# Four edits in the opening steps of a fused attention, FFN and routed-expert kernel, and one rule on when the routing search may advance

## The chip, the cores and the metric

The kernel runs on one core of one Trainium2 chip. The metric is the device time of one execution in microseconds, as the median of several runs; below 0.2% (about 1.6 us here) two kernels can hardly be told apart. A core has TensorE (PE; its weight loads are shown as PEld), VectorE (DVE), ScalarE (ACT), GpSimd (POOL) and SyncE (SP), each with its own instruction stream in program order. They wait for one another by semaphores. Matmul results land in PSUM banks; everything else lies in SBUF.

## The reference, cut to what matters

```python
# 1. retention attention: q, k, v are (4, 8, 576, 64)
ret = (scale * q @ k.T) * Dmat            # Dmat: decay gamma**(i-j) below the diagonal
x = (ret @ v)                             # -> x: 2304 tokens x 512
# 2. a dense FFN over all tokens
h = x @ w_in                              # 512 -> 2048
g = h * np.tanh(np.log1p(np.exp(h)))
x = g @ w_out                             # 2048 -> 512
# 3. routing: 8 experts with room for 288 tokens each
logits = x @ w_gate
order = np.argsort(-logits.flatten())     # greedy: the best (token, expert) pair first,
                                          # skipping taken tokens and full experts
# 4. each expert's FFN on its own 288 rows
out[mask] = np.maximum(x[mask] @ w1[e], 0.0) @ w2[e]    # 512 -> 1024 -> 512
```

## The kernel before, in words

**First part.** `first_part` runs attention and the dense FFN together. The tokens are cut into 9 blocks of 256 and the 2048 features into 16 tiles; a step is one pair (block, tile). Every product is made from a high and a low half of each operand: `ff_h` does 12 products into `ph` (4 contraction tiles, each xh·winh, xh·winl, xl·winh, L323). Then a step walks through short passes: `ff_a1` (three ACT passes on `d`, L332 to L334, and a DVE product `rs`, L340), `ff_a2` (DVE reciprocal, L345), `ff_b1` (DVE product `u`, L350), `ff_b2` (DVE, L358) and `ff_b3` (high half `gh` on ACT, L364; low half `gl` on DVE in these steps, L365). Three steps later `ff_y` multiplies by w_out.

**Weights.** They arrive as raw words and are converted, one 128x512 part per step over the first 32 parts, by the methods of `convert`: `x1` (L163) and `c` (L160) on ACT at the end of a step, `x` (L167) and `a` (L172) on DVE at the start of the next, `h` on ACT (L178, the high half `winh`/`woh`), and one step later `l` (L181, the low half `winl`/`wol`) on POOL. `c` writes a tile `y` in SBUF, and `a` combines `y` with the raw words, which also lie in SBUF.

**Attention pieces.** `slots` hangs the attention of the next tokens into the steps. `a_scores(c)` makes the scores of chunk c in two PSUM banks and their decayed copies `pm` (DVE, L228), and scales Q and K in place on POOL (L232, L237). `a_out(c)` multiplies: four products with the state `sd` (L247), eight with `pm` (L252); then the block's input is written as `xh` (ACT, L258) and `xl` (DVE, L259). `a_state(c)` updates the state bank F (L277). PSUM banks A to E are handed out in turn by `bank()`. Step 4 is block 1 with tile 0, the first step that needs block 1's xh and xl, which `a_out(3)` in step 3 completes. Within step 3 the source has, in this order: `x` and `a` of the part in work, `u` of step 2, `ff_a1` of step 3, `gh`/`gl` of step 1, then the slots, then `ff_h` of step 4.

**Second part.** The experts run one after the other, `ph` 0 to 7: 96 products into `hp` (L1336), then 96 into `op` (L1350), all with 288 columns. A planner in the program text keeps an estimated clock of each engine (`clk`) and decides between products which side piece is put in next: `step()`, a piece of the routing search (`cnt` L1045, `full` L1049, `dg` L1055, `tau` L1060, `ind` L728 on DVE; at the end of an expert's search `de` L1064 on PE and a DVE chain from `dm` L1066 to `m0n` L1075), `fill()` (building the row lists), the gather of the next expert's rows, and `transposes(ph + 1, kt)`, four of them (`tps` counts them): three transposes `tp` on PE (L1297, two buffers), then `xth` on ACT (L1310) and `xtl` on DVE (L1314). A `step()` moves the planner's clocks, so where it is taken decides what the planner does later too.

Of the kernel before, what the change touches and what calls it, by code (L numbers as in the profile page):

```python
# [7 lines left out]
F32 = mybir.dt.float32  # L8
# [4 lines left out]
U32 = mybir.dt.uint32  # L13
U16 = mybir.dt.uint16
I64 = mybir.dt.int64
AF = mybir.ActivationFunctionType
ALU = mybir.AluOpType

P = 128
B, H, S, D = 4, 8, 576, 64  # L20
N, DM, FF, E, F = 2304, 512, 2048, 8, 1024
# [9 lines left out]
MID = (2, 3, 5, 8, 8, 9, 11, 14)  # L31
JOIN = (9, 14)
YL = 3
NF = FF // P


# [45 lines left out]
def first_part(ctx, tc, att, att_ht, att_hn, dtab, qtab, ktab, stab, wi, wo, wgb, ydram, L, constants, cst, begin, grid):  # L82
    nc = tc.nc
# [9 lines left out]
    D_ = big.tile([P, 2, 4, P], F32, name="dt")  # L93
# [49 lines left out]
    class convert:  # L143
# [8 lines left out]
            self.i = done[0]  # L152
            done[0] += 1

        def c(self):
            if self.i in (2, 3):
                self.t = spare[:, self.i % 2 * 512:][:, :512]
            else:
                self.t = cvs[self.i % 2]
            nc.scalar.activation(self.t, self.w1.bitcast(F32), AF.Copy, scale=2.0 ** -112)  # L160

        def x1(self):
            nc.scalar.activation(self.w0, self.top, AF.Copy, scale=2.0 ** -13, bias=-0.4999)  # L163
# [1 line left out]
        def x(self):  # L165
            w0 = self.w0
            nc.vector.scalar_tensor_tensor(w0, self.w1, 0x80000000, w0, op0=ALU.bitwise_and,  # L167
                                           op1=ALU.bitwise_or)

        def a(self):  # L170
            t = self.t.bitcast(U32)
            nc.vector.scalar_tensor_tensor(t, t, 3, self.w0, op0=ALU.logical_shift_left,  # L172
                                           op1=ALU.bitwise_or)
            if self.i not in (6, 7):
                fetch()
# [18 lines left out]

    att_tags = ["A", "B", "C", "D", "E"]
    turn = [0]

    def bank(tag=None):  # L200
# [93 lines left out]
    def micro(n):  # L294

        out = []
        for ci in chunks_of(n):
            if n == 3:
                out.append([lambda ci=ci: a_scores(ci, (0,))])
                out.append([lambda ci=ci: a_scores(ci, (1,))])  # L300
            else:
                out.append([lambda ci=ci: a_scores(ci)])
            out.append([lambda ci=ci: a_out(ci)])
            out.append([lambda ci=ci: a_state(ci),
                        lambda ci=ci: load_chunk(ci + 2) if ci + 2 < len(CHUNKS) else None])
        return out
# [8 lines left out]
    def ff_h(n, f, i):  # L315
        xh, xl = x_block(n)
        if i % 2 == 0:
            hbank[0] = psum.tile([P, 2, TB], F32, tag=("ph0", "ph1")[i // 2 % 2], name="ph")
        ph = hbank[0][:, i % 2, :]
        k = 0  # L320
        for kt in range(KT):
            for w, x in ((winh, xh), (winl, xh), (winh, xl)):
                nc.tensor.matmul(ph, w[f][:, kt, :], x[:, kt, :], start=(k == 0), stop=(k == 11))  # L323
                k += 1
        q2[n, f] = ph
# [160 lines left out]
    slots = {}  # L486
# [14 lines left out]
        nc.tensor.matmul(state[0][:, hp % 4, :], SD[:, 0, :], SD[:, 0, :], start=True, stop=True)  # L501
    unread = psum.tile([P, 2, TB], F32, tag="ph1", name="unread")

    def fill(n):
        for k in range(n):
            nc.tensor.matmul(unread[:, 0, :P], D_[:, 0, 0, :], D_[:, 0, 1, :], start=True, stop=True)

    a_scores(0)
    fill(2)
# [50 lines left out]
    for i in range(len(steps) + YL):  # L560
        new = i < len(steps)
        if not i or new and not_yet(i):
            ff_h(*steps[i], i)
        if i == 20:
            constants()
        if i == 62:
            stage.__exit__(None, None, None)
            late = tc.tile_pool(name="late", bufs=1)
            WG = late.__enter__().tile([P, E, DM], F32, name="WG")
            nc.sync.dma_start(WG, wgb)  # L570
        if now:
            now.x()
            now.a()
        if old:
            old.l()
        if new:
            n, f = steps[i]
            alone = bool(now or old)
            eng = nc.vector if alone else nc.gpsimd
            if not alone:  # L580
                for x in slots.get(i, []):
                    x()
            if i and steps[i - 1] in inv:
                ff_b1(*steps[i - 1], nc.vector)
            ff_a1(n, f, i, alone)
            if i > 1:
                ff_b3(*steps[i - 2], eng)
            if alone:
                for x in slots.get(i, []):
                    x()  # L590
            if now:
                now.h()
            if alone or i == len(steps) - 2:
                ff_h(*steps[i + 1], i + 1)
            while behind:
                behind.pop()()
            ff_a2(n, f)
            if i:
                ff_b2(*steps[i - 1])
            if eng is not nc.vector:  # L600
                ff_b1(n, f, nc.vector if i == len(steps) - 1 else eng)
        if i == len(steps) - 1:
            ff_b2(n, f)
            ff_b3(*steps[i - 1], nc.gpsimd)
            ff_b3(n, f, nc.vector)
        old, now = now, None
        if nxt and i in CONV:
            now, nxt = nxt, convert() if done[0] < len(parts) else None
            now.x1()
            now.c()  # L610
        for k in range(2 if i % 4 == 0 or TAIL <= i < POP2 else 1):
            if idle:
                idle.pop(0)()
        if late and i > TAIL + BEGIN and not idle:
            late = late.__exit__(None, None, None)
            soon.extend(begin())
        if i >= YL:
            ff_y(*steps[i - YL], i)
# [18 lines left out]
RM = (0, 0.1)  # L637
# [165 lines left out]
def second_part(ctx, tc, L, ydram, wx, cst, out, st, fast, L0=None):  # L803
# [5 lines left out]
    nc = tc.nc  # L809
# [642 lines left out]
    for ph in range(E):  # L1452
# [12 lines left out]
        for i, _ in enumerate(ffn(ph)):  # L1465
            clk["pe"] += MM
            rush()
            hurry = fills and ph + 1 not in IDX
            if hurry:
                if fills[0][0] or clk["dve"] <= clk["pe"] + HB:  # L1470
                    fill()
            elif len(COMP) < ph + 3 and clk["route"] + RM[ph > 0] <= clk["pe"]:
                step()
            elif fills and clk["dve"] <= clk["pe"] + 0.7:
                fill()
            if gat and ph + 1 in IDX:
                gather(ph + 1)
                clk["pool"] = max(clk["pool"], clk["pe"], clk["dve"] + 0.9) + 3.5
                there = clk["pool"] + 2.3
                gat = False  # L1480
            fetch()
            if fetched and fetched[0][0] <= ph + 1 and fetched[0][3] + DD <= clk["pe"] \
                    and clk["pool"] <= clk["pe"] + 1.0 \
                    and (not hurry or max(clk["pool"], clk["pe"] + 1.0) + 2.35 <= clk["gather"] + DG):
                split()
            if i in DUE:
                pieces(ph, DUE[i])
            if i in todo:
                todo[i]()
            if nxt and not gat and i >= due and tps < KT and clk["pe"] >= there:  # L1490
                transposes(ph + 1, tps)
                tps += 1
                due = i + min(20, max(6, (188 - i) // max(KT - tps, 1)))
# [145 lines left out]
```

## Time and profile before

| what | value |
|---|---|
| median of 3 runs | 793.83 us (793.38 to 793.94) |
| the profiled execution, whole | 800.43 us |
| its span (first to last instruction) | 798.6 us |
| PE busy | 756.1 us, 95% |
| DVE busy | 541.0 us, 68% |
| ACT busy | 435.2 us, 54% |
| POOL busy | 483.3 us, 61% |
| mean granted clock of TensorE | 0.977 |

The profiled execution is 6.60 us longer than the median; 1.83 us of it lies outside the span. A share of 95% is an average over stages. So the profile is read by stretches: in a stretch where PE isn't full, another engine sets the pace, and in the others PE does. A row of the timeline gives the start in us, the duration, the engine, the line, the operation, out<-in with the shapes, the count, and in brackets the idle time of that engine before the row with what ended it. Instructions on one engine overlap a little, so the distance of two starts is the cost of the first one.

### The profile page before, as it was taken

How to read it: one execution, taken by the hardware profiler on the slowest of the kernel's cores; microseconds unless marked ns; L12 is line 12 of the kernel's file. 1: busy time of each engine (PE TensorE's matmuls, PEld its weight loads, DVE VectorE, ACT ScalarE, POOL GpSimd, SP SyncE). 2: the span in 40 equal slices, each digit the busy share in tenths (PEclk: the TensorE clock that was granted, in tenths of full speed). 3: DMA queues.
4: the chain of work that ended last, by engine and by line, in shares of the span. 5: the costliest groups of instructions: out<-in, count | busy, mean ns of one | idle time of the engine just before them, and what ended most of it. 6: DMA issues, size and time to landing. Idle time of an engine off the chain costs nothing.

```text
span 798.6 us, 16299 instructions
## 1 busy us (share of the span) xinstructions
PE 756.1 (95%) x6163; PEld 698.4 (87%) x6163; DVE 541.0 (68%) x1260; ACT 435.2 (54%) x944; POOL 483.3 (61%) x546
## 2 busy tenths in 40 slices
PE   7799899999999999999999999949999999999995
PEld 6687777898989998989889999839899989999995
DVE  5999998555646897997988976666566754542220
ACT  4789997545445545555555564414444644644631
POOL 2643333555546676676675665327688988978921
PEclk9999999999999999999999999958999999999998
DMA  9556442010333200212010000045466567556411
GB/s 344 201 180 217 158 146 75 28 31 24 106 99 114 80 27 27 81 54 80 16 38 27 2 27 2 1 160 189 145 190 189 172 200 221 164 165 218 136 31 32
DMA packets 27380, 87.79 MB, mean 110 GB/s; under 512 B 4464, under 2 KB 5616, under 8 KB 27168
## 3 DMA queue, kind: packets, MB, share of 16 engines
q1 hardware_dynamic: 24160, 77.06, 29.7%
q0 software_dynamic: 3136, 9.64, 3.7%
q8 instruction: 49, 0.80, 0.4%
q14 instruction: 35, 0.29, 0.1%
HBM read 77.25 MB, written 9.44 MB: 109 GB/s over the span
## 4 chain that ended last, share of the span: by engine, by line
PE 72%; DVE 13%; issue 7%; POOL 2%; ACT 2%; DMA 2%; another core or an unknown queue 0%; POOLq 0%; SPq 0%; DVEq 0%; ACTq 0%
PE ph L323 20%; PE hp L1336 10%; PE op L1350 10%; PE b_E L417 8%; PE b_F L417 8%; DVE rs L345 3%; DVE y L172 2%; DVE raw L167 2%; PE cnt L1045 1%; PE b_A L223 1%; DVE u L350 1%; POOL wxl L876 1%; PE b_D L252 1%; PE b_E L453 1%; PE b_F L453 1%
## 5 line engine op out<-in xcount | busy, mean ns | idle before, releaser
L323 PE MATMUL ph<-xh,winh 128*128 128x256 f32 x576 | 164.9, 286 | 8.4 <-ACT d L332 5.4
L323 PE MATMUL ph<-xl,winh 128*128 128x256 f32 x576 | 160.7, 279 | 0.8 <-DVE xl L259 0.8
L323 PE MATMUL ph<-xh,winl 128*128 128x256 f32 x576 | 160.8, 279 | 0.0
L876 POOL TENSOR_TENSOR wxl<-wraw,wxh 128x1024 fp32r<-128x1024 f32 x63 | 149.3, 2394 | 9.0 <-ACT wxh L874 7.5
L323 PEld LDWEIGHTS ph<-xh,winh 128*128 128x128 f32 x576 | 108.5, 188 | 23.8 <-ACT d L332 9.9
L365 POOL TENSOR_TENSOR gl<-u,gh 128x256 fp32r<-128x256 f32 x114 | 88.9, 780 | 62.9 <-ACT gh L364 62.2
L332 ACT ACTIVATE d<-ph 128x256 f32<-128x256 f32 x144 | 54.9, 381 | 128.8 <-PE ph L323 114.5
L323 PEld LDWEIGHTS ph<-xh,winl 128*128 128x128 f32 x576 | 108.6, 189 | 4.0
L345 DVE RECIPROCAL u<-u 128x128 f32<-128x128 f32 x113 | 107.7, 953 | 3.9
L323 PEld LDWEIGHTS ph<-xl,winh 128*128 128x128 f32 x576 | 108.6, 189 | 1.3 <-DVE xl L259 1.3
L340 DVE TENSOR_TENSOR u<-d 128x128 f32<-128x128 f32 x113 | 53.4, 473 | 60.6 <-ACT d L334 60.0
L352 POOL TENSOR_TENSOR u<-d,u 128x128 f32<-128x128 f32 x112 | 51.7, 461 | 58.8 <-DVE u L345 58.8
L333 ACT ACTIVATE d<-d,half_b 128x256 f32<-128x256 f32 x144 | 73.5, 511 | 4.7
L874 ACT ACTIVATE wxh<-wraw 128x1024 fp32r<-128x1024 f32 x64 | 67.3, 1053 | 13.6 <-DMA wraw<-in_wx_dram 13.6
L353 POOL TENSOR_TENSOR u<-d,u 128x128 f32<-128x128 f32 x112 | 68.8, 614 | 8.8
L334 ACT ACTIVATE d<-d 128x256 f32<-128x256 f32 x144 | 60.2, 418 | 4.5
L364 ACT ACTIVATE gh<-u 128x256 fp32r<-128x256 f32 x144 | 58.1, 403 | 5.4 <-DVE u L358 4.4
L374 DVE SCALAR_TENSOR_TENSOR scr<-y,WG 128x512 bf16<-128x512 f32 x64 | 56.4, 881 | 0.4
L1327 DVE SCALAR_TENSOR_TENSOR htl<-hp,hth 128x288 fp32r<-128x288 f32 x64 | 29.1, 455 | 35.1 <-ACT hth L1339 34.2
L358 DVE SCALAR_TENSOR_TENSOR u<-u,ph 128x256 f32<-128x256 f32 x144 | 52.0, 361 | 0.0
L1339 ACT ACTIVATE hth<-hp 128x288 fp32r<-128x288 f32 x64 | 26.1, 409 | 43.4 <-PE hp L1336 34.5
L1336 PE MATMUL hp<-xth,wxh 128*128 128x288 f32 x256 | 49.4, 307 | 0.0
(299 smaller groups left out, 1874.6 us busy)
## 6 DMA issues: line engine op xcount, KB each, us to landing
wraw<-in_wx_dram SPq DMA_DIRECT2D x64, 512.0 KB, 4.4
att<-in_att_dram SPq DMA_DIRECT2D x32, 512.0 KB, 5.8
raw<-in_wi_dram SPq DMA_DIRECT2D x16, 512.0 KB
raw<-in_wo_dram SPq DMA_DIRECT2D x16, 512.0 KB, 3.2
ydram<-y SPq DMA_DIRECT2D x9, 512.0 KB, 2.8
WG<-in_wgb_dram SPq DMA_DIRECT2D x1, 2048.0 KB
att<-in_att_ht_dram SPq DMA_DIRECT2D x4, 256.0 KB
att<-in_att_hn_dram SPq DMA_DIRECT2D x4, 256.0 KB
```

Source lines behind the costliest of these rows:

```text
L323: nc.tensor.matmul(ph, w[f][:, kt, :], x[:, kt, :], start=(k == 0), stop=(k == 11))
L333: nc.scalar.activation(df, df, AF.Square, bias=half_b, scale=-0.5)
L334: nc.scalar.activation(df, df, AF.Copy, bias=0.5, scale=0.5)
L345: nc.vector.reciprocal(r, r)
L353: eng.tensor_mul(u[:, 0, :], d[:, 1, :], r)
L364: nc.scalar.activation(gh, g, AF.Copy)
L365: eng.tensor_sub(gl, g, gh.bitcast(F32))
L417: nc.tensor.matmul(py[n][t], g[:, t * P:(t + 1) * P], w[f], start=(f == 0 and w is woh and g is gh), stop=(f == NF - 1 and g is gl))
L874: nc.scalar.activation(hi, raw, AF.Copy)
L876: rest = lambda eng: eng.tensor_sub(lo, raw, hi.bitcast(F32))
L1336: nc.tensor.matmul(hp, W[ft // 2][w][:, s], x[:, kt, :], start=(k == 0), stop=(k == 11))
L1350: nc.tensor.matmul(op, W[4 + dt][w][:, s], h[:, ft, :], start=(k == 0), stop=(k == 23))
```

## The change

Five edits, four in the first part:

1. A constant `SOON = 3` names the step. The PSUM bank E is kept out of the rotation of the attention pieces until step 4, so that the early pieces take A to D.
2. `c(aside)`: at the end of steps 0 and 1 ACT writes the converted part to PSUM bank E instead of `y`. In steps 1 and 2 DVE's `a` then reads one input from PSUM and one from SBUF, and writes `y`.
3. The K scaling of chunk 3 goes from POOL to DVE.
4. In step 3, `ff_a1` and the slots (`a_out(3)`, `a_state(3)`, a load) stand ahead of `u` and `gh`/`gl`; six products that nobody reads, into bank E, stand between the slots and `ff_h` of step 4.
5. In the second part `step()` is not taken while `ph == 0` and at least one of the second expert's four transposes has been put in.

```diff
@@ -31,6 +31,7 @@
 YL = 3
+SOON = 3
@@ -152,12 +153,13 @@
-        def c(self):
+        def c(self, aside=False):
             if self.i in (2, 3):
                 self.t = spare[:, self.i % 2 * 512:][:, :512]
             else:
                 self.t = cvs[self.i % 2]
-            nc.scalar.activation(self.t, self.w1.bitcast(F32), AF.Copy, scale=2.0 ** -112)
+            self.s = bank("E").rearrange("p a b -> p (a b)") if aside else self.t
+            nc.scalar.activation(self.s, self.w1.bitcast(F32), AF.Copy, scale=2.0 ** -112)
@@ -168,8 +170,7 @@
         def a(self):
-            t = self.t.bitcast(U32)
-            nc.vector.scalar_tensor_tensor(t, t, 3, self.w0, op0=ALU.logical_shift_left,
+            nc.vector.scalar_tensor_tensor(self.t.bitcast(U32), self.s.bitcast(U32), 3, self.w0, op0=ALU.logical_shift_left,
                                            op1=ALU.bitwise_or)
@@ -194,7 +195,7 @@
-    att_tags = ["A", "B", "C", "D", "E"]
+    att_tags = ["A", "B", "C", "D"]
@@ -299,7 +300,7 @@
-                out.append([lambda ci=ci: a_scores(ci)])
+                out.append([lambda ci=ci: a_scores(ci, eng=nc.vector if ci == 3 else nc.gpsimd)])
@@ -501,9 +502,9 @@
-    def fill(n):
+    def fill(n, to=unread[:, 0, :P]):
         for k in range(n):
-            nc.tensor.matmul(unread[:, 0, :P], D_[:, 0, 0, :], D_[:, 0, 1, :], start=True, stop=True)
+            nc.tensor.matmul(to, D_[:, 0, 0, :], D_[:, 0, 1, :], start=True, stop=True)
@@ -561,6 +562,8 @@
+        if i == SOON + 1:
+            att_tags.append("E")
@@ -577,17 +580,22 @@
-            if not alone:
-                for x in slots.get(i, []):
-                    x()
+            todo = list(slots.get(i, []))
+            if i == SOON:
+                ff_a1(n, f, i, alone)
+            if not alone or i == SOON:
+                while todo:
+                    todo.pop(0)()
             if i and steps[i - 1] in inv:
                 ff_b1(*steps[i - 1], nc.vector)
-            ff_a1(n, f, i, alone)
+            if i != SOON:
+                ff_a1(n, f, i, alone)
             if i > 1:
                 ff_b3(*steps[i - 2], eng)
-            if alone:
-                for x in slots.get(i, []):
-                    x()
+            while todo:
+                todo.pop(0)()
+            if i == SOON:
+                fill(6, bank("E")[:, 0, :])
@@ -607,7 +615,7 @@
-            now.c()
+            now.c(i < 2)
@@ -1469,7 +1477,7 @@
-            elif len(COMP) < ph + 3 and clk["route"] + RM[ph > 0] <= clk["pe"]:
+            elif len(COMP) < ph + 3 and clk["route"] + RM[ph > 0] <= clk["pe"] and (ph or not tps):
                 step()
```

Lines of the changed kernel stand 1 or 2 higher in the first part and 8 higher in the second. Three places show the moved instructions.

On DVE, steps 2 and 3 of the first part, before (`raw` and `y` are the converted part, `rs` and `u` the gate, `att` chunk 3's K):

```order
L167 SCALAR_TENSOR_TENSOR raw<-raw 128x512
L172 SCALAR_TENSOR_TENSOR y_153<-y_153,raw 128x512
L350 TENSOR_TENSOR u<-d,rs 128x256
L340 TENSOR_TENSOR rs<-d 128x128
L365 TENSOR_TENSOR gl<-u,gh 128x256
L228 TENSOR_TENSOR pm<-b_E,dt 128x512
L228 TENSOR_TENSOR pm<-b_A,dt 128x512
L345 RECIPROCAL rs<-rs 128x128
L358 SCALAR_TENSOR_TENSOR u<-u,ph 128x256
L167 SCALAR_TENSOR_TENSOR raw<-raw 128x512
L172 SCALAR_TENSOR_TENSOR y_153<-y_153,raw 128x512
L350 TENSOR_TENSOR u<-d,rs 128x256
L340 TENSOR_TENSOR rs<-d 128x128
L365 TENSOR_TENSOR gl<-u,gh 128x256
L259 TENSOR_TENSOR xl<-b_B,xh 128x4x128
```

The same stretch of DVE after:

```order
L169 SCALAR_TENSOR_TENSOR raw<-raw 128x512
L173 SCALAR_TENSOR_TENSOR y_153<-b_E,raw 128x512
L351 TENSOR_TENSOR u<-d,rs 128x256
L341 TENSOR_TENSOR rs<-d 128x128
L366 TENSOR_TENSOR gl<-u,gh 128x256
L229 TENSOR_TENSOR pm<-b_B,dt 128x512
L229 TENSOR_TENSOR pm<-b_C,dt 128x512
L238 TENSOR_TENSOR att<-att,kt 128x512
L346 RECIPROCAL rs<-rs 128x128
L359 SCALAR_TENSOR_TENSOR u<-u,ph 128x256
L169 SCALAR_TENSOR_TENSOR raw<-raw 128x512
L173 SCALAR_TENSOR_TENSOR y_153<-y_153,raw 128x512
L341 TENSOR_TENSOR rs<-d 128x128
L260 TENSOR_TENSOR xl<-b_D,xh 128x4x128
L351 TENSOR_TENSOR u<-d,rs 128x256
```

The first `y` pass reads the bank E, the K scaling stands behind the two `pm`, and `xl` stands ahead of `u` and `gl` where it stood behind both.

On PE, the end of the first expert (its last `op` products, then the second expert's first `hp`; `tp` are the second expert's transposes), before:

```order
L1297 MATMUL tp<-c_ident,xg 128x96 x3
L1350 MATMUL op<-hth,wxl_6887 128x288
L1055 LDWEIGHTS c_ones
L1055 MATMUL dg<-cl,c_ones 128x1
L1350 MATMUL op<-hth,wxl_6887 128x288 x3
L1350 MATMUL op<-htl,wxh_6886 128x288 x2
L1297 MATMUL tp<-c_ident,xg 128x96 x3
L1350 MATMUL op<-htl,wxh_6886 128x288 x6
L1297 MATMUL tp<-c_ident,xg 128x96 x6
L1336 MATMUL hp<-xth,wxh_7029 128x288
L1045 LDWEIGHTS ind
L1045 MATMUL cnt<-oh,ind 66x8
```

The same place on PE after:

```order
L1305 MATMUL tp<-c_ident,xg 128x96 x3
L1358 MATMUL op<-hth,wxl_6896 128x288 x4
L1358 MATMUL op<-htl,wxh_6895 128x288 x2
L1305 MATMUL tp<-c_ident,xg 128x96 x3
L1358 MATMUL op<-htl,wxh_6895 128x288 x6
L1305 MATMUL tp<-c_ident,xg 128x96 x6
L1344 MATMUL hp<-xth,wxh_7038 128x288
L1063 LDWEIGHTS c_ones
L1063 MATMUL dg<-cl,c_ones 128x1
L1344 MATMUL hp<-xth,wxh_7038 128x288 x3
```

The `dg` of the search moves from before the turns' end to behind the first `hp` product, and with it `tau`, `ind` (DVE) and the next 18 `cnt` products.

On PE, the end of the second expert (`tp` are now the third expert's transposes, `de` the end of the third expert's search), before, where the four turns stand at distances of some 13 products:

```order
L1297 MATMUL tp<-c_ident,xg 128x96 x3
L1350 MATMUL op<-hth,wxh_7327 128x288
L1064 LDWEIGHTS c_ones
L1064 MATMUL de<-full,c_ones 128x8
L1350 MATMUL op<-hth,wxh_7327 128x288 x3
L1350 MATMUL op<-hth,wxl_7328 128x288 x8
L1350 MATMUL op<-htl,wxh_7327 128x288
L1297 MATMUL tp<-c_ident,xg 128x96 x3
```

The same place on PE after:

```order
L1305 MATMUL tp<-c_ident,xg 128x96 x3
L1358 MATMUL op<-htl,wxh_7352 128x288
L1072 LDWEIGHTS c_ones
L1072 MATMUL de<-full,c_ones 128x8
L1358 MATMUL op<-htl,wxh_7352 128x288 x4
L1305 MATMUL tp<-c_ident,xg 128x96 x9
L1344 MATMUL hp<-xth,wxh_7401 128x288 x4
```

The first turn stands some 40 products later than before, and the other three behind one another right ahead of the third expert's first product. On DVE the four `xtl` (L1322) stand together behind `dm` to `m0n`; before, one stood ahead, and the others apart. From the fifth expert on, the order of the second part is the one before. The POOL stream has one instruction less (K), SP's is the same.

## Rows read from the trace of the kernel before

**Rows 1.** Windows: stretch, length, busy PE, PEld, DVE, ACT, POOL; PEclk, DMA, GB/s.

```profile
60.00:80.00 20.00, 18.54 (x138) 15.70 (x137) 19.47 (x41) 18.81 (x43) 7.01 (x7) 1.00 0.60 215
140.00:160.00 20.00, 20.00 (x130) 17.88 (x130) 11.97 (x23) 11.21 (x28) 11.62 (x20) 1.00 0.08 28
```

**Rows 2.** Timeline of DVE, steps 1 to 3.

```profile
14.01 0.70 DVE L237 TENSOR_TENSOR att<-att,kt 128x512 f32<-128x512 f32 x1
...
22.18 0.68 DVE L228 TENSOR_TENSOR pm<-b_B,dt 128x512 f32<-128x512 f32 x1
...
25.05 1.58 DVE L172 SCALAR_TENSOR_TENSOR y<-y,raw 128x512 uint32<-128x512 uint32 x1
...
28.93 0.69 DVE L167 SCALAR_TENSOR_TENSOR raw<-raw 128x512 uint32<-128x512 uint32 x1
29.73 1.61 DVE L172 SCALAR_TENSOR_TENSOR y<-y,raw 128x512 uint32<-128x512 uint32 x1
31.27 1.26 DVE L350 TENSOR_TENSOR u<-d,rs 128x256 f32<-128x256 f32 x1
32.45 1.35 DVE L340 TENSOR_TENSOR rs<-d 128x128 f32<-128x128 f32 x1
...
35.26 0.94 DVE L345 RECIPROCAL rs<-rs 128x128 f32<-128x128 f32 x1
...
37.79 0.42 DVE L350 TENSOR_TENSOR u<-d,rs 128x256 f32<-128x256 f32 x1
38.12 0.29 DVE L340 TENSOR_TENSOR rs<-d 128x128 f32<-128x128 f32 x1
```

**Rows 3.** Timeline of POOL, the same steps.

```profile
22.08 1.32 POOL L232 TENSOR_TENSOR att<-att,qt 128x512 f32<-128x512 f32 x1
...
24.36 1.73 POOL L181 TENSOR_TENSOR winl<-spare,winh 128x512 fp32r<-128x512 f32 x1
...
28.94 1.85 POOL L232 TENSOR_TENSOR att<-att,qt 128x512 f32<-128x512 f32 x1 [0.28 <-POOL wol L181]
30.74 1.51 POOL L237 TENSOR_TENSOR att<-att,kt 128x512 f32<-128x512 f32 x1
32.21 1.45 POOL L181 TENSOR_TENSOR wol<-y,woh 128x512 fp32r<-128x512 f32 x1
```

**Rows 4.** Timeline of PE: products that waited, in steps 1 and 3.

```profile
23.45 1.16 PE L247 MATMUL b_D<-att,sd 128*128 128x128 f32 x8 [1.19 <-POOL att L232]
...
34.80 0.43 PE L252 MATMUL b_B<-pm,att 128*64 128x128 f32 x2 [2.46 <-DVE pm L228]
...
39.40 0.39 PE L323 MATMUL ph<-xl,winh 128*128 128x256 f32 x1 [0.46 <-DVE xl L259]
```

**Rows 5.** Windows behind PE's waits of 1.19 and 2.46 us; columns as above.

```profile
23.40:26.00 2.60, 2.55 (x40) 2.39 (x40) 2.50 (x4) 1.32 (x4) 2.60 (x2) 1.00 0.90 359
...
36.00:37.50 1.50, 1.50 (x23) 1.50 (x21) 1.40 (x4) 0.52 (x2) 0.00 (x0) 0.50 0.00 0
```

**Rows 6.** Timelines of PE, then DVE, at the first expert's end.

```profile
573.54 0.47 PE L1297 MATMUL tp<-c_ident,xg 96*128 96x96 f32 x3 [0.64 <-DVE xtl L1314]
```

```profile
572.24 0.77 DVE L728 TENSOR_TENSOR ind<-dv,tau 128x594 bf16<-128x594 f32 x1
```

**Rows 7.** Timelines of PE, then DVE, at the second expert's end.

```profile
599.88 0.18 PE L1064 MATMUL de<-full,c_ones 66*128 66x8 bf16 x1
...
600.40 1.22 PE L1350 MATMUL op<-hth,wxl 128*128 128x288 f32 x8
```

```profile
600.11 0.17 DVE L1066 TENSOR_REDUCE dm<-de 128x1 f32<-128x8 f32 x1 [1.04 <-PE de L1064]
...
601.19 0.45 DVE L1314 TENSOR_TENSOR xtl<-tp,xth 128x288 fp32r<-128x288 f32 x1
```

**Rows 8.** Timeline of PE and a window, early in the fourth expert's phase.

```profile
649.97 0.17 PE L1064 MATMUL de<-full,c_ones 66*128 66x8 bf16 x1 [1.93 <-DVE full L1049]
...
650.00:653.40 3.40, 3.40 (x17) 3.37 (x17) 2.52 (x13) 2.14 (x4) 2.44 (x4) 0.53 0.40 116
```

## The prediction, made before the changed kernel had run

> **What bounds the kernel now.** I read the windows first. Between 60 and 80 us DVE is busy 19.47 of 20 us and ACT 18.81, while PE has gaps, 18.54; between 140 and 160 us PE is busy all 20 and DVE only 11.97 [rows 1]. So the early steps are paced by DVE with ACT close behind, and all later ones by PE. An opening that brings DVE's chain forward by some time therefore passes that time on to the end; one that only fills PE's gaps there does not. Then I read the timelines of DVE and POOL side by side. A pass of DVE with two SBUF inputs of 128x512 takes 0.70 us when POOL is idle (the row at 14.01) [rows 2]. `a` takes 1.58 at 25.05 and 1.61 at 29.73, and ends where a POOL pass ends: `winl` runs 24.36 to 26.09, Q 28.94 to 30.79 [rows 2, 3]. Q, which began while DVE's `x` (28.93 to 29.62) was running, took 1.85 instead of 1.32. So each blocks the other for a whole pass, whichever began first. `u` at 31.27 and `rs` at 32.45 take 1.26 and 1.35 in the same way, and 0.42 and 0.29 later, when POOL has stopped [rows 2]. A pass that reads PSUM and SBUF isn't held: `pm` at 22.18 takes 0.68 while Q runs from 22.08 [rows 2, 3]. PE pays for this with 2.46 us ahead of `a_out(3)` and 0.46 ahead of the first product with xl [rows 4]. Last I read the ends of the first two experts, where edit 5 works [rows 6, 7].
>
> **Edits 2 and 1: `a` reads PSUM.** The nearest row for the new form is `pm`, unheld at 0.68; the farthest is today's 1.61. I take 0.69, since `pm` is the same mix of sources beside the same kind of POOL pass. The Trainium skill, "VectorE: DVE Perf Modes", section "The TRN2 errata", lists a PSUM source at 120 fixed cycles against 58 at 0.96 GHz; as an estimate that makes two passes 0.13 us longer and the time 0.13 us worse. The trace shows no such difference: `pm` takes 0.68, the SBUF form 0.70 [rows 2], so nothing is added for it.
>
> The replay, step by step:
> - Step 1: `a` would end 0.9 earlier, but `u` behind it, which began when `a` had ended (26.6), has two SBUF inputs and is held until `winl` ends at 26.09. What is left is 0.5, and `x` of step 2 starts at 28.43 instead of 28.93.
> - Step 2: POOL's Q can begin when `x` lets go, near 29.1, and ends 1.3 later, at 30.4 (1.32 when unheld) [rows 3]. `a` runs 29.2 to 29.9, not held. `u` is held by Q until 30.4 and ends some 0.25 behind it, near 30.6 (before: 32.53, where POOL's K ended at 32.25). `rs` takes 0.29 instead of 1.35. Then `gl` (0.4) and the two `pm` (0.6 apart each) as before. The reciprocal that started at 35.26 could start at 32.3: 3.0 us earlier.
> - **Edit 3.** K on DVE adds 0.60 to 0.70 to this chain (the row at 14.01) [rows 2], and POOL's `wol` (1.28 to 1.45) may hold it a little, 0.2. It takes K's 1.51 off POOL [rows 3], which DVE no longer has to wait for. The reciprocal then starts near 33.05: a gain of **2.2**.
>
> **Edit 4.** `a_out(3)` starts when the second `pm` ends, near 32.3 instead of 35.3, so PE's wait of 2.46 goes. `xl` now stands ahead of `u` and `gl`, 0.42 and 0.4 of work that it no longer waits for. DVE is back to back there, so moving passes about doesn't shorten its chain: the gain at the next reciprocal stays 2.2. ACT's `gh` and `xh` follow those DVE and PE rows, and come earlier with them. The six products have 128 columns each, at most 0.14 us a piece by the eight in 1.16 at 23.45 [rows 4], so 0.6 to 0.9 in all. They lie in a gap: with some 1.7 us (an estimate from the same row, for more but smaller products) PE would be done with `a_out(3)` and `a_state(3)` near 34.0. xl comes later: `rs` at 38.12 started 2.86 behind the reciprocal at 35.26 [rows 2]; without `u` (0.33) ahead and with `rs` itself (0.2), xl starts 2.7 behind the new reciprocal, at 35.8, and ends near 36.4. So the six cost nothing while xl is late; if it came by 34.0, they would cost all of their 0.9. What is left of the gap is a pause of about 1.4 us ahead of the third product. PE's granted clock was 1.00 in the stretch of the 1.19 us wait and 0.50 behind the 2.46 us one [rows 4, 5]. The new pause is nearer the first, so I take full clock; at half clock for about 2 us PE loses 1 us, partly hidden since DVE paces. The opening then gives 2.2, with bounds of 0.8 (half clock and `gl` held) and 3.0 (K free).
>
> **Edit 5, end of the first expert.** Before, PE waits 0.64 us ahead of the fourth turn for an `xtl`, which stood behind the `ind` pass of 0.77 at 572.24 [rows 6]. Without search pieces between the turns this `ind` is gone from there and `xtl` follows its `xth` directly. I leave 0.2 for the short chain from `xth`, and let the 18 `cnt` products behind move without loss: **-0.5** (bounds 0 and -0.8). What is not searched here must be searched later; in the later experts PE is the bound and the search passes hide beside its products, so the pieces cost what they cost now.
>
> **Edit 5, end of the second expert.** The planner's clocks have moved: the third expert's four turns stand together, 39 products later. On DVE their `xtl` stand behind `dm` to `m0n`. That chain runs from `de` at 599.88 to the `xtl` at 601.19: 1.31 us [rows 7]. Before, it ran beside a dozen products, eight of which take 1.22 (the row at 600.40) [rows 7], and PE did not wait. After, only four products (0.6) stand between `de` and the nine transposes, and there are two buffers, so the third turn waits for the first `xtl`: 1.31 + 0.45 (a pass) - 0.6 - 0.2 (three transposes) = 1.0 (0.96). The fourth turn waits 0.2 more, the first products of the third expert 0.2. Against it stand some 0.3 for interruptions saved. Net **+1.0** (bounds +0.6 and +1.7). The gather stands as many products ahead of its first turn as before, so I give it nothing.
>
> **Waits behind `full`.** `de` at 649.97 waited 1.93, and the clock after it was 0.53 over 3.4 us [rows 8], a loss of 1.6. Such waits come while POOL issues gathers. Edit 5 reorders the search there. Whether they go, stay, or appear elsewhere can't be read from the order; bounds -3.5 and +3.5, and I take 0, as the nearest row of the same instruction, `de` at 599.88, waited for nothing.
>
> **Sum.** -2.2 - 0.5 + 1.0 = **-1.7**. The profiled execution becomes 800.43 - 1.7 = 798.7. It stood 6.6 above the median, and I keep that distance: 793.83 - 1.7 = **792.1**.
>
> **Rivals.**
> - **The race (792.9 to 793.3).** Where DVE's `gl` or K begins just after POOL's `wol`, it is held for up to 1.2 us: by the replay `gl` starts only some 0.2 us before `wol` does. The Trainium skill, "SBUF — State Buffer", section "Who interferes with whom", says that whoever begins first has the shared ports for the whole instruction, which the rows at 25.05 and 28.94 agree with. The opening then gives 1.0, and with -0.5 and +1.0 the sum is -0.5: 793.3. For it: 0.2 us is less than the replay's error. Against: `gl` goes first as drawn.
> - **The change doesn't do it (793.5).** `a` from PSUM is still held, as its second input lies in SBUF. Then edits 2 and 3 give only what K's move gives, 1.51 of POOL less against 0.6 of DVE more, about 0.8; -0.8 - 0.5 + 1.0 = -0.3. Against: `pm` at 22.18.
> - **Slower: `de` waits late (795.6).** At the second expert's end `de` now has the four turns behind it. If `full` releases it as late as at 649.97, PE waits 1.93 and loses 1.6 to the clock: -1.7 + 3.5 = +1.8. It decides from a wait of some 1.7 us, where the sum turns positive with the clock's loss. For it: the row at 649.97. Against: `de` at 599.88, in the same place of the expert, had no wait.
> - **The late wait goes (788.6).** The reorder takes the wait of 649.97 away, and it is there in timed runs too: -1.7 - 3.5 = -5.2. For it: that `de` moves. Against: the profiled execution is 6.6 longer than the median, and waits of this kind may be part of that.
>
> **How the numbers follow.** Forecast 0.49 (own range 791.2 to 793.1), race 0.16, not done 0.08, late `de` 0.12, wait gone 0.15. About 0.2%, 1.59 us, is what a measurement can tell from no change: the marks are 792.24 and 795.42. The forecast lies near the first mark: 0.29 of it faster, 0.20 same. Race 0.01 faster, 0.15 same; not done 0.08 same; late `de` 0.10 slower, 0.02 same; wait gone 0.15 faster. Together 0.45 faster, 0.45 same, 0.10 slower. The range from 788.6 to 794.8 leaves out half of the last rival (0.07) and most of the late `de` (0.10).
>
> **What would show it.** Right: in the trace after, `a` from `b_E` takes about 0.7 in steps 1 and 2 beside POOL's passes, the reciprocal of step 3 starts near 33.0, `xl` ends near 36.5, and PE has no wait over 1.6 us with the clock at 1.00 ahead of `ff_h` of step 4; no wait over 0.3 ahead of the second expert's turns; about 1 us ahead of the third expert's third turn. Wrong: `a` at 1.5 (not done), `gl` or K at over 1.2 (race), a clock near 0.5 behind the third expert's turns (late `de`), no `de` wait near 650 us (wait gone). And if the opening's 2.2 stands at 40 us but is no longer there at 140 us, my reading of the bound is wrong.

## The result: 0.54% slower, and where the profile puts it

The changed kernel takes 798.88 us (median of 20 runs, 795.1 to 801.84), the kernel before 794.29 (20 runs, 793.17 to 796.46). The ratio is 1.0054 (95% interval 1.0041 to 1.0067): slower by some 4.3 us, where 792.1 was forecast. The runs of the changed kernel lie in two bunches: 7 of 20 between 795.1 and 796.1, 13 between 798.0 and 801.8. The kernel before has no such second bunch.

The profiled execution after took 799.79 us (span 798.0), 0.6 less than the profiled one of before, and must not be read that way: before's profiled execution carried late waits that the others don't have (below). So the comparison is made from the starts of each step.

The opening did what it was drawn for. These are rows of DVE's timeline after, answering [rows 2]:

```profile
24.79 0.69 DVE L173 SCALAR_TENSOR_TENSOR y<-b_E,raw 128x512 uint32<-128x512 uint32 x1
...
28.97 0.69 DVE L173 SCALAR_TENSOR_TENSOR y<-b_E,raw 128x512 uint32<-128x512 uint32 x1
...
31.96 0.72 DVE L238 TENSOR_TENSOR att<-att,kt 128x512 f32<-128x512 f32 x1
32.61 0.94 DVE L346 RECIPROCAL rs<-rs 128x128 f32<-128x128 f32 x1
```

`a` with a PSUM source is not held (0.69 instead of 1.58 and 1.61), K on DVE costs 0.65, and the reciprocal that started at 35.26 starts at 32.61: 2.65 us earlier. Then DVE's rows, and POOL's beside them, read so:

```profile
35.34 0.69 DVE L260 TENSOR_TENSOR xl<-b_D,xh 128x512 fp32r<-128x512 f32 x1
35.94 0.42 DVE L351 TENSOR_TENSOR u<-d,rs 128x256 f32<-128x256 f32 x1
36.27 1.52 DVE L366 TENSOR_TENSOR gl<-u,gh 128x256 fp32r<-128x256 f32 x1
...
40.24 0.97 DVE L351 TENSOR_TENSOR u<-d,rs 128x256 f32<-128x256 f32 x1
41.13 1.39 DVE L341 TENSOR_TENSOR rs<-d 128x128 f32<-128x128 f32 x1
42.45 1.26 DVE L366 TENSOR_TENSOR gl<-u,gh 128x256 fp32r<-128x256 f32 x1
...
54.95 1.52 DVE L351 TENSOR_TENSOR u<-d,rs 128x256 f32<-128x256 f32 x1
56.39 1.13 DVE L341 TENSOR_TENSOR rs<-d 128x128 f32<-128x128 f32 x1
57.44 1.48 DVE L366 TENSOR_TENSOR gl<-u,gh 128x256 fp32r<-128x256 f32 x1
```

```profile
35.96 1.55 POOL L182 TENSOR_TENSOR wol<-y,woh 128x512 fp32r<-128x512 f32 x1 [3.82 <-ACT woh L179]
39.71 1.22 POOL L233 TENSOR_TENSOR att<-att,qt 128x256 f32<-128x256 f32 x1 [2.19 <-issue]
41.07 1.30 POOL L182 TENSOR_TENSOR winl<-y,winh 128x512 fp32r<-128x512 f32 x1
42.33 1.10 POOL L238 TENSOR_TENSOR att<-att,kt 64x512 f32<-64x512 f32 x1
...
54.37 1.81 POOL L233 TENSOR_TENSOR att<-att,qt 128x512 f32<-128x512 f32 x1 [1.05 <-PE b_D L224]
56.15 1.22 POOL L238 TENSOR_TENSOR att<-att,kt 128x512 f32<-128x512 f32 x1
57.33 1.31 POOL L182 TENSOR_TENSOR wol<-y,woh 128x512 fp32r<-128x512 f32 x1
```

Each of these seven DVE passes needs 0.28 to 0.42 us when it stands alone (the `u` at 35.94, and `rs` at 38.12 in [rows 2]). Seven times one begins while a POOL pass runs, and it ends 0.15 to 0.29 us after that pass has ended: 36.27 behind `wol`, 40.24 to 42.45 behind Q, `winl` and K, 54.95 to 57.44 behind Q, K and `wol`. Their excess is 1.10 + 0.55 + 1.11 + 0.84 + 1.10 + 0.85 + 1.06 = 6.6 us. In the kernel before, the three passes of the last group were through when Q came (DVE, then POOL):

```profile
55.02 0.42 DVE L350 TENSOR_TENSOR u<-d,rs 128x256 f32<-128x256 f32 x1
55.36 0.29 DVE L340 TENSOR_TENSOR rs<-d 128x128 f32<-128x128 f32 x1
55.56 0.42 DVE L365 TENSOR_TENSOR gl<-u,gh 128x256 fp32r<-128x256 f32 x1
```

```profile
56.05 1.32 POOL L232 TENSOR_TENSOR att<-att,qt 128x512 f32<-128x512 f32 x1 [2.50 <-PE b_D L223]
```

In this stretch before, only two `a` passes were held, by 0.66 and 0.91:

```profile
45.63 1.35 DVE L172 SCALAR_TENSOR_TENSOR y<-y,raw 128x512 uint32<-128x512 uint32 x1
...
59.04 1.60 DVE L172 SCALAR_TENSOR_TENSOR y<-y,raw 128x512 uint32<-128x512 uint32 x1
```

Put side by side, the starts of the reciprocals of the steps (the time before, and after minus before) follow these holds one by one:

| reciprocal before at | after minus before | what happened in between |
|---|---|---|
| 35.26 | -2.65 | opening, as drawn |
| 39.26 | -1.54 | `gl` at 36.27 held, 1.10 |
| 43.6 | +0.72 | `u`, `rs`, `gl` at 40 to 43 held, 2.50 |
| 48.8 | -0.07 | before's own held `a`, 0.66 |
| 57.12 | +2.92 | `u`, `rs`, `gl` at 55 to 58 held, 3.01 |
| 61.43 | +2.01 | before's own held `a`, 0.91 |
| 65.4 | +3.46 | half clock of PE behind its wait of 3.77 |
| 152.3 | +4.06 | 0.30 and 0.35 more in two steps by 90 us (not followed), then unchanged |

The line before the last is PE's price, in its timeline, and in windows (columns as in [rows 1]):

```profile
59.58 0.50 PE L418 MATMUL b_C<-woh,gh 128*128 128x512 f32 x1 [3.77 <-DVE pm L229]
```

```profile
61.00:63.20 2.20, 2.20 (x10) 2.01 (x9) 2.10 (x6) 0.94 (x2) 0.00 (x0) 0.50 0.17 69
...
60.00:80.00 20.00, 19.12 (x133) 16.40 (x132) 17.82 (x38) 15.69 (x36) 5.29 (x5) 0.91 0.52 186
140.00:160.00 20.00, 20.00 (x128) 17.93 (x127) 11.95 (x24) 11.14 (x28) 10.70 (x19) 1.00 0.07 27
```

The bank that PE wants next holds scores which `pm` can't read before `gl` is through. PE stands still for 3.77 us and comes back at 0.50 of its clock, so that between 60 and 80 us DVE is no longer full (17.82 of 20, where [rows 1] had 19.47): the bound went over to a slowed PE, and another 1.5 us are lost. DVE's row for it is the `xl` that waits for ACT's `xh`, which waits for PE:

```profile
68.30 0.69 DVE L260 TENSOR_TENSOR xl<-b_E,xh 128x512 fp32r<-128x512 f32 x1 [1.37 <-ACT xh L259]
```

From 140 us on PE is full, and the difference stays between 4.0 and 4.4 us up to 475 us. Behind that the granted clock of this execution falls for some 3 us (0.91 and 0.89 in the windows 484 to 488 and 488 to 500 us), which before's doesn't, and the first part ends 5.0 us behind.

In the second part the only wait of PE over 0.5 us between 560 and 700 us is this one:

```profile
PE tp L1305 <- DVE xtl L1322: 0.8, 1, 0.8
```

It is the expected wait of the third expert's turns; the 0.64 of [rows 6] is gone. The four late waits at `dg` and `de` of before's profiled execution, 4.4 us in sum, with the clock's loss of 1.6 behind the longest [rows 8], are absent. They are absent as well from the profile of the opening alone (next section), which has the old search rule: from 555 us to the end it takes 6.5 us less than before's profiled execution. No other profiled execution here has them. So they belonged to that one, not to the old rule, and they account for its being 6.6 us above its median.

### The profile page after: what moved, and what is told of

Read it like the earlier page. It is cut to its first block, busy times and chain, and to the rows that moved or that the text cites. A ratio compares the mean times of both kernels' runs of the same rounds, so it can differ in the third digit from the quotient of the medians.

```text
span 798.0 us, 16327 instructions
## 1 busy us (share of the span) xinstructions
PE 758.3 (95%) x6175; PEld 699.6 (88%) x6175; DVE 546.4 (68%) x1261; ACT 434.8 (54%) x944; POOL 481.6 (60%) x545
## 4 chain that ended last, share of the span: by engine, by line
PE 71%; DVE 13%; issue 7%; ACT 3%; POOL 3%; DMA 2%; POOLq 0%; SPq 0%; DVEq 0%; ACTq 0%
PE ph L324 19%; PE hp L1344 11%; PE op L1358 10%; PE b_E L418 8%; PE b_F L418 7%; DVE rs L346 2%; PE cnt L1053 1%; DVE raw L169 1%; POOL wxl L884 1%; DVE y L173 1%; DVE u L351 1%; PE b_A L224 1%; PE b_F L454 1%; PE b_E L454 1%; PE b_D L253 1%
## 5 line engine op out<-in xcount | busy, mean ns | idle before, releaser
L1344 PE MATMUL hp<-xtl,wxh 128*128 128x288 f32 x256 | 47.9, 303 | 0.0
```

The lines of the kernel that those rows point to most:

```text
L1344: nc.tensor.matmul(hp, W[ft // 2][w][:, s], x[:, kt, :], start=(k == 0), stop=(k == 11))
```

## The experiments

The theory: **DVE passes that run into POOL passes** in the steps behind the opening give back its gain and more, since the opening moved DVE, PE and POOL against each other. The rival: the second part, through the **search rule**, costs the time. The expectations call the two later groups of held passes steps 5 and 8; counted by their reciprocals they are steps 4 and 7. All ratios are to the kernel before in runs on the same chip; distances to the changed kernel are between medians, across chips on which the kernel before measured 794.3 to 794.7.

### The opening alone, and the search rule alone

The first kernel takes back edit 5:

```diff
-            elif ... clk["route"] + RM[ph > 0] <= clk["pe"] and (ph or not tps):
+            elif ... clk["route"] + RM[ph > 0] <= clk["pe"]:
```

> Edits 1 to 4 alone, the search rule as before. Theory 'collisions': the opening's gain of 2.7 us at the fourth step is given back, because seven DVE passes (gl, u, rs) run into POOL passes between 36 and 59 us and are held 6.7 us in sum; so this kernel is slower than before by 3.5 to 4.5 us (797.8 to 798.8), and a step at 140 us starts about 4 us later than before. Rival 'search rule': the 4.6 us come from the second part, and the opening alone gives 791.5 to 794.5.

Measured: 799.93 us against 794.72, ratio 1.0054 (1.0037 to 1.0071). The profile holds the same seven passes (`gl` at 36.70 with 1.52, and so on to `gl` at 57.87 with 1.49); the reciprocal of 152.3 stands at +5.64. The median lies above the range expected. In the profile 0.4 of the excess over the changed kernel's +4.06 is there from the start, and 1.1 more comes where PE runs at half clock, here from 60 to 66 us.

The second adds only edit 5 to the kernel before:

> Edit 5 alone, the opening as before. Theory 'collisions': near nothing, -0.5 to +1.0 us against before (793.8 to 795.3). Rival 'search rule': +3.5 to +5 us (797.8 to 799.3).

Measured: 794.71 against 794.72, ratio 1.0004 (0.9993 to 1.0015). The whole loss is the opening's; the rival falls.

This profile also shows something about the kernel before, whose opening it has. Its DVE, then POOL:

```profile
28.79 1.81 DVE L167 SCALAR_TENSOR_TENSOR raw<-raw 128x512 uint32<-128x512 uint32 x1
...
31.97 0.41 DVE L350 TENSOR_TENSOR u<-d,rs 128x256 f32<-128x256 f32 x1
32.31 0.28 DVE L340 TENSOR_TENSOR rs<-d 128x128 f32<-128x128 f32 x1
```

```profile
28.77 1.28 POOL L232 TENSOR_TENSOR att<-att,qt 128x512 f32<-128x512 f32 x1 [0.25 <-POOL wol L181]
```

In [rows 2, 3] `x` began 0.01 us ahead of POOL's Q, and later `u` and `rs` were held. Here Q begins 0.02 ahead, `x` is held instead (1.81), and `u` and `rs` are free. The reciprocal of 35.26 starts at 34.05, 1.2 us earlier, and this lasts to 152 us. So the opening before is a race too: against this outcome the change's opening gains 1.4 us and not 2.65. Which outcome is the more frequent isn't shown.

### Undo the order of step 3

```diff
-            if i == SOON:
-                ff_a1(n, f, i, alone)
-            if not alone or i == SOON:
+            if not alone:
...
-            if i != SOON:
-                ff_a1(n, f, i, alone)
+            ff_a1(n, f, i, alone)
...
-            if i == SOON:
-                fill(6, bank("E")[:, 0, :])
```

> The changed kernel with edit 4 undone (step 3 in its old order, no six products); edits 1, 2, 3, 5 stay. gl of step 3 stands ahead of xl again, so it should begin before POOL's wol and take 0.4 instead of 1.5. Theory 'collisions': the first held pass goes (about 1.1 us), and the passes behind it fall differently against POOL's; so the time differs from the changed kernel's by over 1 us, most likely 1 to 4 us below 798.9. Rival 'search rule': as the changed kernel within 0.7 us, or slower by the 0.5 us that PE loses at xl.

Measured: 793.91 us, ratio 0.9988 (0.9978 to 0.9999), 5 us below the changed kernel, more than the 1 to 4 expected. No `gl`, `u` or `rs` is held behind 30 us; only before's own two `a` are. The lead of 2.46 lasts to the second reciprocal and falls to 0.94 at the third, for another reason, which the version with 14 products takes up. This edit undoes two things, the order and the six products; the version with six products, further down, undoes the order alone.

### Delay PE: more work, less time

The scores of the chunk of step 7 are made three times into the same banks, 16 products more:

```diff
-        for hp in range(4):
+        for hp in [0, 1, 2, 3] * (3 if ci == 6 else 1):
             for s, t in ts:
```

> The changed kernel with 16 more products on PE in step 7 (the scores of one chunk are made three times into the same bank, which changes no value), so that POOL's Q pass of that chunk starts about 1.8 us later, behind DVE's gl. Theory 'collisions': u, rs and gl of step 8 take 0.4, 0.3, 0.4 instead of 1.5, 1.1, 1.5, and PE's wait of 3.8 us ahead of its bank C goes; the time falls by 2 to 3.5 us against the changed kernel (795.4 to 796.9), though PE has more to do. Rival 'search rule', or any account without the collisions: 0 to +1.8 us against the changed kernel.

Measured: 795.65 us, ratio 1.0012 (1.0003 to 1.0021): 3.2 us below the changed kernel, with more to do on PE. POOL's Q, which has to wait for the scores, and DVE:

```profile
54.77 0.42 DVE L351 TENSOR_TENSOR u<-d,rs 128x256 f32<-128x256 f32 x1
55.10 0.29 DVE L341 TENSOR_TENSOR rs<-d 128x128 f32<-128x128 f32 x1
55.30 0.42 DVE L366 TENSOR_TENSOR gl<-u,gh 128x256 fp32r<-128x256 f32 x1
```

```profile
56.14 1.32 POOL L233 TENSOR_TENSOR att<-att,qt 128x512 f32<-128x512 f32 x1 [3.02 <-PE b_D L224]
```

Q starts at 56.14 instead of 54.37, behind `gl`, and 1.52, 1.13, 1.48 become 0.42, 0.29, 0.42. PE's wait of 3.77 is gone too. The held passes up to 43 us stay.

### The changed kernel again: a natural experiment

> The changed kernel again beside the two above, on the same chip: 4 to 5 us above before, with a wider spread than before's (the seven held passes are races of starts within some 0.3 us, so some runs fall out otherwise). In its profile gl at 36 us is held and u, rs, gl at 55 us, if the time is near 800; if the time is near 795.5, the three at 55 us should be free.

Measured: 799.1 us, ratio 1.0063 (1.0045 to 1.0081). Its profiled execution fell into the lower bunch, 795.72. Up to 43 us it holds the same four passes as the other one; at 55 us it holds none:

```profile
54.87 0.41 DVE L351 TENSOR_TENSOR u<-d,rs 128x256 f32<-128x256 f32 x1
55.20 0.28 DVE L341 TENSOR_TENSOR rs<-d 128x128 f32<-128x128 f32 x1
55.40 0.42 DVE L366 TENSOR_TENSOR gl<-u,gh 128x256 fp32r<-128x256 f32 x1
```

```profile
55.59 1.40 POOL L233 TENSOR_TENSOR att<-att,qt 128x512 f32<-128x512 f32 x1 [2.33 <-PE b_D L224]
```

Q came 1.2 us later, behind `gl`, because PE was later. The windows say why, first of the execution of 799.79, then of the one of 795.72:

```profile
47.00:48.00 1.00, 1.00 (x7) 0.87 (x6) 1.00 (x4) 1.00 (x2) 0.35 (x1) 1.00 0.19 37
48.00:49.00 1.00, 1.00 (x11) 0.56 (x11) 1.00 (x4) 0.97 (x4) 0.94 (x1) 1.00 0.72 262
```

```profile
47.00:48.00 1.00, 1.00 (x6) 1.00 (x6) 1.00 (x5) 1.00 (x3) 0.44 (x1) 0.50 0.28 45
48.00:49.00 1.00, 1.00 (x4) 0.81 (x3) 1.00 (x4) 0.97 (x4) 0.85 (x1) 0.50 0.77 254
```

In the faster execution the granted clock (third column from the end) was halved from 46 to 49.5 us, behind gaps of PE at 42 to 46 us that the slower one has as well (its wait there is 0.77, the other's 0.80). The slower clock went with the shorter run: it put the scores, and so Q, behind `gl`, as the 16 products did. So in the executions profiled the two bunches are the same race with two outcomes. Why the clock fell in one of them and not in the other is not shown.

### Take the POOL passes away

`a_scores` returns ahead of Q and K for the chunks of steps 4 and 7:

```diff
+        if ci in (4, 6):
+            return
         if s0 > 0:
             nc.gpsimd.tensor_mul(qT, qT, Q_[:, :, :n])
```

> The changed kernel without POOL's Q and K passes of the two chunks whose scores stand in steps 4 and 7 (those chunks' values are left unscaled, so that part of the computation is missing). Theory 'collisions': u, rs and gl of step 8 are not held (about 3.0 us less), those of step 5 only by winl (1 to 2.5 us less); the time is 3 to 5.5 us below the changed kernel, 793.4 to 795.9. Without the collisions as cause: within 0.7 us of the changed kernel, as POOL is not the bound of these steps.

This version leaves the two chunks' values unscaled. Measured: 793.11 us, ratio 0.9985 (0.9972 to 0.9997): 5.8 us below the changed kernel, a little beyond the range. In its profile only the `gl` of 36 us stays held (1.52), and the lead is 2.85 at the reciprocal of 65.4. Later it loses some 2 us beside a PE wait of 2.5 for ACT, which I have not followed.

### The six products, and K, each undone alone

Without the line `fill(6, bank("E")[:, 0, :])`:

> The changed kernel without the six unread products; the new order of step 3 stays. PE then pauses about 2.2 us ahead of xl instead of 0.7. Theory: the pause costs the clock (half for 3 to 4 us, as behind the 2.46 us wait before), so PE reaches the next scores about 1.5 us later, and POOL's Q and K there fall elsewhere against u, rs and gl; the time differs from the changed kernel's by over 1 us, more likely down (795 to 798) than up. Rival 'the products cost their own time': 0 to 1.4 us less than the changed kernel, with the same passes held.

Measured: 793.52 us (7 of 10 runs between 792.6 and 793.9, three at 798.3 to 802.1), ratio 1.0019 (0.9991 to 1.0047), which the three long runs pull up. PE waits 1.6 us for xl instead of 0.67, and in the profile neither group behind `gl` is held: the lead is 1.91 at 57 us. The median lies below the range that I gave. `gl` at 36 us is held here too (1.51), so this hold alone doesn't bring the others. The clock is 0.50 from 37 to 39 us, and Q of step 4 starts at 41.06 instead of 39.71, when `gl` of that step (40.59, 0.42) is through. The three long runs were not profiled; they suggest that here too a race decides.

With K of chunk 3 back on POOL (`a_scores(ci)`):

> The changed kernel with edit 3 undone: K of chunk 3 back on POOL. K then runs near 30.0 to 31.1 us and holds the gl of step 2 by about 0.6; DVE is spared K's 0.65. Theory: the distance of gl and wol in step 3 is unchanged, gl is held again, and the seven held passes stay; the time is the changed kernel's within 1.2 us. Rival 'K on DVE is what breaks the rhythm': 3 us or more below the changed kernel.

Measured: 796.74 us (794.2 to 803.2), ratio 1.0047 (1.0024 to 1.0071), 2.1 below the changed kernel by the medians, beyond the 1.2 that I allowed, but only 0.6 by the ratios, whose intervals overlap: the time doesn't tell whether K's place matters. In its profile `rs` and `gl` are held at 31 and 32 us (1.13, 1.49) by K and `wol`, then `gl` at 38.34 and the group at 42 to 44.5, but not the group of step 7. So the seven held passes did not stay, as I had expected: I had left out that the last group depends on PE's distance as well.

### A version that beats both

In the kernel with the old order of step 3 the lead fell from 2.46 to 0.94 because PE paused ahead of xl and came back slowed, so that DVE had to wait for PE and ACT. Its window, then the same one with 14 unread products in the pause:

```profile
37.00:41.00 4.00, 4.00 (x16) 3.46 (x16) 3.17 (x7) 3.11 (x8) 0.42 (x1) 0.57 0.05 11
```

```profile
37.00:41.00 4.00, 4.00 (x40) 3.39 (x39) 3.63 (x9) 3.56 (x9) 0.71 (x2) 1.00 0.05 12
```

```diff
             while todo:
                 todo.pop(0)()
+            if i == SOON:
+                fill(14, bank("E")[:, 0, :])
             if now:
                 now.h()
```

> An attempt at a better version: edits 1, 2, 3, 5 with step 3 in its old order, and 14 unread products ahead of the next block's first product, so that PE has no pause of over 0.5 us ahead of xl. Without them that kernel lost 1.6 us of its lead because PE ran at half clock from 37.4 to 40.9 us and DVE waited for ACT and PE (0.7 and 0.8). Theory: the clock stays at 1.00 and the lead of 2.4 us is kept through step 5, unless chunk 4's Q pass, now earlier, holds u or gl there: 791.5 to 793 if not, 793.5 to 795.5 if so.

Measured: 792.66 us, ratio 0.9984 (0.9972 to 0.9995), 1.3 us below before by the ratio, less than the 0.2% that two kernels need to be told apart. The clock is 1.00, and the lead is 2.56 at the reciprocal of 35.26 and 2.34 at that of 65.4. Q of step 7 runs at 53.71, behind a `gl` of 0.41 at 53.21.

With 6 products in place of 14:

> The version with 14 products, with 6. PE then pauses about 1.7 us ahead of xl. Theory: it is the pause that costs the clock, so with 6 products the clock falls again behind xl, though for less than the 3.5 us without products; the lead falls from 2.3 to between 0.9 (as with none) and 2.3: 792.7 to 794. If the number of products does not matter, within 0.3 us of 792.7.

Measured: 793.6 us, ratio 0.9987 (0.9977 to 0.9998). From the changed kernel this version differs in the order of step 3 alone, and it is 5.3 us shorter. `gl` of step 3 begins at 35.96, ahead of `wol` at 36.24, and takes 0.42; Q of step 4 comes at 40.61, when `gl` of that step (40.21) has all but ended; no `gl`, `u` or `rs` is held behind 30 us. The reason that I gave fails: PE pauses 1.3 us there, and the profile shows the clock at 1.00 and the lead at 2.36 as with 14. Its profiled execution falls behind the other only near 482 us, by 1.5 us, where PE is full and nothing waits; the windows there:

```profile
482.00:483.00 1.00, 1.00 (x7) 1.00 (x6) 0.00 (x0) 0.00 (x0) 0.62 (x2) 0.50 0.00 0
483.00:484.00 1.00, 1.00 (x7) 1.00 (x7) 0.00 (x0) 0.00 (x0) 0.00 (x0) 0.50 0.00 0
```

The clock was halved for some 3 us. The same happens between 480 and 500 us in four of the thirteen profiled executions and not in the others, so it can't be put down to the products, and what the eight more of them bring is not shown.

With 14 products and without edit 5:

> The better version without edit 5 (the search rule as before), so edits 1, 2, 3, the old order of step 3 and 14 products. Between two undisturbed profiles, the opening alone and the changed kernel, edit 5 cost 1.0 us from the second expert on, after a gain of 0.7 at the first expert's end; alone it measured 0.0 to +0.3 us. So: 791.5 to 793, the same as with edit 5 or up to 1.0 us less. If it is over 0.5 us more, edit 5 is worth keeping.

Measured: 791.99 us (9 runs, 791.03 to 792.89), ratio 0.9971 (0.9959 to 0.9983), the best of all: 2.3 us below before and 6.9 below the changed kernel. Its interval overlaps that of the version with edit 5 (0.9972 to 0.9995), so what edit 5 costs there is not clear of the noise.

## Why the prediction was wrong

- **Right, the opening's own sum.** `a` from PSUM at 0.69 as taken, not held; K at 0.65 on DVE as taken; the reciprocal at 32.61 against a forecast of 33.05, a gain of 2.65 against 2.2. (Against the other outcome of the opening before, which one profile couldn't show, the gain is 1.4.) xl ended at 36.0 instead of 36.4. PE's pause ahead of xl was 0.67 instead of 1.4, as the six products take 1.4 us and not 0.6 to 0.9; the clock stayed at 1.00, as taken. The rival that `a` from PSUM is still held fell. One reading was loose: `a` does not end where the POOL pass ends but 0.54 and 0.55 us later (26.63 against 26.09, 31.34 against 30.79); the sum did not rest on it.
- **The step that failed.** "An opening that brings DVE's chain forward by some time therefore passes that time on to the end": this treats DVE's chain behind the opening as of fixed length. Its length depends on where POOL's passes fall, and [rows 2, 3] said so: behind the opening 6.6 us of holds came in and 1.6 went out, and a PE wait of 3.77 with half clock added 1.5. The replay ended at `xl`; at the reciprocal behind it the lead still read -1.54; the next 25 us, with eight more POOL passes, were not replayed. The prediction's own sign, a gain that stands at 40 us and is gone at 140, came. It was to mean that the bound was misread; but DVE does set the pace there, save for the few us behind that PE wait, and it is the length of its chain that was misread.
- **The race, right in kind and wrong in size.** The rival named `gl` against `wol` with 0.2 us between them, and this was lost: `wol` began 0.3 us ahead and the hold cost 1.1. It was priced as one hold. Undoing the order alone is worth 5.3 us, since the two later groups, six passes, go with it. They need a second thing, though: without the six products `gl` is lost all the same and in the profile both groups are free. That whoever begins first holds the other for a whole instruction (the Trainium skill, "SBUF — State Buffer", section "Who interferes with whom") agrees with every held pass here, and with `x` and Q, of which the one that began 0.01 or 0.02 us earlier held the other; what the sum lacked was how often it would strike.
- **Edit 4's place.** I wrote that moving passes about doesn't shorten DVE's chain. It lengthened it: `gl`, put behind xl, stands 0.6 us later against `wol` than in the old order, and this is what carries it past the start of `wol` (35.87 against 36.15 in the old order, 36.27 against 35.96 in the new one).
- **The six products** were to cost nothing while xl is late. They do keep the clock at 1.00, but that brings the scores, and with them POOL's Q of step 4, forward into `u` (Q at 39.71, `u` at 40.24); without them Q came at 41.06. A cost by way of a third engine stood in no term of the sum.
- **Edit 5.** -0.5 + 1.0 was forecast; alone it measured +0.3 us by the ratio (-0.6 to +1.2), and 0.7 between the medians of the versions with 14 products, which isn't clear of the noise. Between the profiles of the opening alone and the changed kernel it gains 0.7 at the first expert's end, and from there to the end loses 1.7, a net 1.0 worse. PE's wait at the third expert's turns is 0.84, forecast 1.0.
- **The late waits** were given nothing, which was right for the median: they occur in no other profile. The rival that let one of them go, and the one that put one at the second expert's end, both fell.

## What to carry to other kernels

When a stretch is paced by an engine whose passes another engine can hold, its length isn't a sum of durations: replay both engines to the end of that stretch, not to the end of the edit, and look at every start within some 0.3 us of the other's. Finishing one engine's work earlier can be a loss if it brings a blocking pass of a third engine forward; a delay on the engine that isn't the bound is a cheap test of that, and may be the cure. Profile the kernel before more than once: here one profile showed one of two outcomes of its opening, and waits that it alone had. Where run times come in two bunches, take a profile of each and look for the first row that differs.

## What the runs showed that I had not expected

PE's granted clock differed between executions of one program: PE at half clock from 46 to 49.5 us went with a run 4.1 us shorter of the same program, and 16 products that change nothing took 3.2 us off its median. Near 482 to 500 us it was halved in four of thirteen profiled executions beside a full PE, at a cost of about 1.5 us. One execution of the kernel before carried some 6 us of waits in its second part that no other profiled execution of this case has; as the only one shown beforehand, it made these waits look like a property of the kernel.
